# Banded attention feeding a gated feed-forward: product with v joined to a later pair's scores, ungated weight loads, a table of rank shifts

## The chip, the cores and the metric

One Trainium2 chip, one core of it. The metric is device time in microseconds (us) of one launch, the median of the runs shown. One further execution was taken by the profiler; all rows come from that one.

## What is computed

Attention over 4 batches, 8 heads, 768 positions and head size 64, with a band (128 positions back) and 4 sink positions, followed by a gated feed-forward on 3072 tokens:

```python
scores = scale * np.matmul(q, k.transpose(0, 1, 3, 2))
keep = is_sink | in_window          # pos < 4, or 0 <= row - col < 128
a = softmax(where(keep, scores, -1e9))
x = (a @ v)  as [3072, 512]         # 8 heads of 64 side by side
out = (sigmoid(x @ w_gate) * (x @ w_val)) @ w_out     # 512 -> 1536 -> 512
```

The feed-forward's operands are each cut into a rounded part and a rest, so that a product takes three matrix multiplies (high by high, high by rest, rest by high). The weights arrive as 64-bit floats and are decoded on the chip.

## The kernel before, in words

**Order of the work.** `Plan` (from line 270) is a list scheduler that runs when the kernel is built. Each `plan.op` gives a rank (`prio`, lower goes first), the engines that may run it with a cost in ns, and the tiles that it reads and writes. `Plan.run` (299) plays time forward: when an engine is free it takes the waiting operation of lowest rank whose inputs are there and whose tiles have a free buffer (412). What it writes out is a fixed order of instructions for each engine: PE (TensorE), V (VectorE), A (ScalarE), G (GpSimd) and Q (the SP queue, which issues the DMAs in that order). On the chip each engine keeps to this order, and an instruction whose input is late holds all behind it. When PE has nothing it puts in filler multiplies with the identity (`warm`).

**Attention** works on pairs of heads and blocks of two 128-row tiles: 4 batches, 3 blocks each, 4 pairs each, 48 pairs in all. `u` counts heads in this order and goes up by two for a pair, so u = 28 is the 29th head. `attend` (841) plans one pair with rank u: three loads (k, q, v, from buffers with three places each), the scores on PE (900), masks and row minimum on V, exponentials on A, normalization on G or V, four transposes on PE (985), a copy on A and two masking selects on G into `wt`, and the product with v on PE (`pv`, 1038), whose two halves are copied by A and added by V into `xr`. Scores and `pv` use the array as four 64x64 tiles (`parts=True`); all else on PE uses it whole. The planner charges 150 and 210 ns for changing between the two and, while it is in tiles, looks first for other such operations. Scores take two PSUM banks of the pool `a`, `pv` takes two, a transpose one; the pool has four (`B_a`, 73).

**After each block** `join` (1068) adds the sinks' part and either cuts the block's 256 tokens into `XH`, `XL` for the first form of the feed-forward (`feed`, blocks 0, 1, 2 and 4, ranks of 10000 and over on PE), or writes it to DRAM (the other eight blocks, `SPILL`). These eight are computed once attention is over, by a second form (`wino`) that needs the banks of pool `a`.

**Weights.** There are 12 slices f, each of three matrices (`weights`, 1223). A matrix is one load of 512 KB into one of four raw buffers (`wst` three, `wsx` one) and a chain over A, V and G (`decode`, 1161). The n-th matrix has rank DS + DR n, that is 6.0 + 0.3 n. `GATES` says at which head a slice may start to load: slice 0 after the normalizer (`guard`, 955) of u = 0, the other eleven after that of u = 6, by a dependence through the marker `OPEN`.

Of the kernel before, what the change touches and what calls it, by code (L numbers as in the profile page):

```python
# [40 lines left out]
SINKU = 2  # L41
# [4 lines left out]
DEEP = 3  # L46
SCALP = -0.5
SKSWAP = 0
GATES = ((2, 1), (8, 11))
MORE_W = 1  # L50
DS = 6.0
DR = 0.3
ALT = 1
SURE = 600.0
# [23 lines left out]
B_w = 2  # L78
B_m = 2
BUFS = {}  # L80

@with_exitstack
def general(ctx, tc, q, k, v, ident, nsk, win, wres, wol_d, out):
# [391 lines left out]
def kernel(  # L475
# [362 lines left out]
            lambda: vs()[2 * NR : 3 * NR], [raw], [vs],  # L838
        )

    def attend(u, b, h, t0, T, XS, PSK):

        prev = 1 if t0 else 0
        L = T + prev
        W = T * 128
        if u == SINKU if b == 0 else h == 0 and t0 == 0:
            sinks(b, u)
        at = (b * NT + t0) * H + h * T
        own = u < 2 * H and u // 2 % 2
# [50 lines left out]
        def scores():  # L900
# [10 lines left out]
                            skip_group_check=True, tile_position=(e * D, c * D),  # L911
                        )

        plan.op(
            u, [("PE", 10 + sum(1.67 * (KW + D if t0 + t else KW) for t in range(T)), scores)],
            [qkT, qr], sc + [P], soon=soon, parts=True,
        )
        for e in range(2):

            def pick(e=e):  # L920
                def tiles(at):
                    x = sc[e]()[:, at + SIDE * (T - n) : at + SIDE * (T - n) + 128]
                    return bass.AP(x.tensor, x.offset, (x.ap[0], (SIDE, n), (1, 128)))

                V.copy_predicated(
                    out=tiles(0), mask=tri.unsqueeze(1).to_broadcast([128, n, 128]), data=tiles(KW)
                )

            n = T if t0 else T - 1
            plan.op(u, [("V", 170.0 + 135.0 * n, pick)], [(MASKS, 3)], [sc[e]])  # L930
            for t in range(T):

                def top(e=e, t=t):
                    V.tensor_tensor_reduce(
                        out=Pv()[:, e, t], in0=sc[e]()[:, t * SIDE : t * SIDE + KW],
                        in1=am[min(t0 + t, 2)], op0=ALU.add, op1=ALU.min, scale=-SCALE,
                        scalar=3.0e38,
                        accum_out=negm_all[:, at + e * T + t : at + e * T + t + 1],
                    )

                def exp(e=e, t=t):
                    A.activation(
                        out=Pv()[:, e, t], in_=Pv()[:, e, t], func=AF.Exp,
                        bias=negm_all[:, at + e * T + t : at + e * T + t + 1], scale=-1.0,
                        accum_out=sums()[:, e * T + t, 0:1],
                    )

                plan.op(
                    u, [("V", 330, top)],
                    [sc[e]] + [(MASKS, x) for x in ((0,), (1, 4), (2, 4))[min(t0 + t, 2)]],  # L950
                    [(P, (e, t))],
                )
                plan.op(u, [("A", 495, exp)], [], [(P, (e, t)), (sums, (e, t))])
# [84 lines left out]
        def pv():  # L1038
            for i, (l, halves) in enumerate(blocks):
# [8 lines left out]
                            tile_position=(z * D, e * D),  # L1048
                        )

        plan.op(
            u, [("PE", 15 + sum(1.67 * max(x[2] for x in hs) for _, hs in blocks), pv)],
            [vt, wt], sides + [(xst, c)], parts=True,
        )
        plan.op(
            u, [("A", act(W, True), lambda: A.copy(out=xs()[:, c], in_=sides[0]()[:, 0:W]))],
            [sides[0]], [(xst, c)],
        )
        plan.op(
            u, [("V", vec(W), lambda: V.tensor_tensor(  # L1060
                out=xs()[:, c], in0=sides[1]()[:, 0:W], in1=xs()[:, c], op=ALU.add
            ))],
            [sides[1]], [(xst, c)],
        )
        if h == H - 2:
            join(u + 1, b, t0, T, XS, psk)

    def join(u, b, t0, T, XS, psk):

        W, vs = T * 128, VSP  # L1070
        spill, g = place[b, t0]
        first = u == H - 1
        bank = (
            lambda: Tile(OS, None, F32, "eO", len(OS)) if first
            else Tile(AS, None, F32, "a", len(AS))
        )
        u -= AHEAD if first else 0
        ts = bank()
        sk = tile([3 * NR, W], F32R, "sk", BUFS["sk"], pa)

        def turn():
            for t in range(T):
                PE.transpose(
                    out=ts()[0:NR, t * 128 : t * 128 + 128],
                    in_=psk()[:, t].rearrange("p h s -> p (h s)"), identity=ident,
                )

        n = turn_of.get("sk", 0)
        turn_of["sk"] = n + 1
        plan.op(u, [("PE", 20 + T * 100, turn)], [psk], [ts, sk]).turn = "sk", n  # L1090
        for i in (0, 2):
            plan.op(
                u, [("A", act(W, True), lambda i=i: A.copy(
                    out=sk()[i * NR : i * NR + NR], in_=ts()[0:NR, 0:W]
                ))],
                [ts], [(sk, i)],
            )
        rest(
            u, W, lambda: sk()[NR : 2 * NR], lambda: ts()[0:NR, 0:W], lambda: sk()[0:NR],
            [ts, (sk, 0)], [(sk, 1)], True,  # L1100
        )
        runs = [] if spill else [[0]]
        for t in range(1, 0 if spill else T):
            if chunk_of[g + t] == chunk_of[g + t - 1]:
                runs[-1].append(t)
            else:
                runs.append([t])
        for i, xst in enumerate(XS):
            xs = lambda xst=xst: xst().rearrange("p (c x) -> p c x", c=2)
            for cc in ((0,), (1,)) if T == 3 else ((0, 1),):  # L1110
                C = len(cc)
                sp = bank()
                spv = lambda sp=sp, C=C: sp()[:, 0 : C * W].rearrange("p (c x) -> p c x", c=C)

                def add(i=i, spv=spv, cc=cc):
                    for c in cc:
                        PE.matmul(
                            spv()[:, c - cc[0]], lhsT=vs()[:, 2 * i + c], rhs=sk(), start=True,
                            stop=True,
                        )  # L1120

                plan.op(u, [("PE", C * mac(W), add)], [vs, sk], [sp])
                mine = [(xst, c) for c in cc]
                cut = slice(cc[0], cc[-1] + 1)
                plan.op(
                    u, [("V", vec(C * W), lambda spv=spv, xs=xs, cut=cut: V.tensor_tensor(
                        out=xs()[:, cut], in0=spv(), in1=xs()[:, cut], op=ALU.add
                    ))],
                    [sp], mine,
                )  # L1130
                if spill:
                    dma(
                        u, 728.0, lambda n=g // 2, i=i, xst=xst: Q.dma_start(out=x_d[n, i], in_=xst()),
                        mine, [(XD, (g // 2, i))],
                    )
                for run in runs:
                    cols = slice(run[0] * 128, run[-1] * 128 + 128)
                    k = (g + run[0]) % RING * 128
                    ts_ = slice(k, k + len(run) * 128)
                    fs = slice(2 * i + cc[0], 2 * i + cc[-1] + 1)  # L1140
                    parts = [(2 * i + c, (g + t) % RING) for t in run for c in cc]
                    x = lambda cols=cols, xs=xs, cut=cut: xs()[:, cut, cols]
                    hi = lambda ts_=ts_, fs=fs: XH()[:, fs, ts_]
                    lo = lambda ts_=ts_, fs=fs: XL()[:, fs, ts_]
                    n = C * len(run) * 128
                    copy(u, n, hi, x, mine, [(XH, p) for p in parts], C == 1 and len(run) % 2)
                    rest(
                        u, n, lo, x, hi, mine + [(XH, p) for p in parts], [(XL, p) for p in parts]
                    )
# [595 lines left out]
                    weights(next(decoded), due)  # L1745

    opened(0)
    u = g = fed = ci = 0
    for b in range(B):
        t0 = 0  # L1750
        for T in AT[b]:
            XS, PSK = [], [None]
            for h in range(0, H, 2):
                attend(u, b, h, t0, T, XS, PSK)
                if u >= MIX0 and (u - MIX0) % MIXD == 0 and (u - MIX0) // MIXD < 2 * NP:
                    mixed(u + 0.5, (u - MIX0) // MIXD)
                for _ in range(2):
                    u += 1
                    opened(u)
            if not place[b, t0][0]:  # L1760
                g += T
            t0 += T
            while ci < len(MT) and fed + sum(MT[ci]) <= g:
                feed(ci, fed, MT[ci])
                fed += sum(MT[ci])
                ci += 1
    for i in range(WT):
        wino(ci + i, 4 * i)
    plan.run(WARM, 218.0, warm)
    wres = {f: [w() if i < 4 else w()[:, 0] for i, w in enumerate(ws)] for f, ws in wres.items()}  # L1770

# [79 lines left out]
```

## Time and profile before

| | us |
|---|---|
| median of 3 runs | 739.62 (739.58 to 740.27) |
| profiled execution | 739.36 |
| its span on the core | 737.6 |
| granted TensorE clock, mean | 1.0 of full speed |

The profiled execution's time exceeds the span by 1.8 us of launch and end. The page's rows give busy time by engine; a start-to-start distance between two PE rows says more about PE than its busy share, since matmuls overlap each other.

### The profile page before, as it was taken

The page shows a single profiled execution, that of the slowest core. Times are in us where ns is not written, and L with a number is a line of the kernel's source. Part 1 is how long each engine was busy: PE and PEld are TensorE (multiplying, and loading weights), DVE is VectorE, ACT ScalarE, POOL GpSimd, SP SyncE. Part 2 cuts the span into 40 slices and gives each one's busy share as a digit, 9 for nine tenths or more (in the row PEclk, how much of TensorE's full clock was granted, in tenths as well). Part 3 has the DMA queues.
Part 4 walks back from the last instruction along what each step waited for, and adds up shares of the span by engine and source line. Part 5 has one row for each costly group of instructions (what it writes and reads, how often), then busy time and mean ns, then how long its engine had stood idle before and what let it go on. Part 6 is the DMA issues. An engine that isn't in the chain of part 4 may idle for free.

```text
span 737.6 us, 16836 instructions
## 1 busy us (share of the span) xinstructions
PE 722.3 (98%) x6264; PEld 646.6 (88%) x6264; DVE 400.9 (54%) x1121; ACT 374.2 (51%) x1029; POOL 430.0 (58%) x433
## 2 busy tenths in 40 slices
PE   7999999999999999999999999999999999999997
PEld 6788787888888888899899999999999999999996
DVE  5999998787868766532242354424543334443231
ACT  6988886566656656522233344433444334343332
POOL 3879887999999646510154455644556445554331
PEclk9999999999999999999999999999999999999999
DMA  8768885666767754432245233453334432353312
GB/s 260 259 224 256 289 277 166 215 188 189 224 211 243 237 156 124 140 118 66 77 128 170 88 100 117 146 171 98 99 114 145 161 112 89 120 149 93 122 44 74
DMA packets 71769, 115.43 MB, mean 156 GB/s; under 512 B 7300, under 2 KB 31876, under 8 KB 71684
## 3 DMA queue, kind: packets, MB, share of 16 engines
q1 hardware_dynamic: 71680, 114.32, 49.5%
q8 instruction: 50, 0.82, 0.4%
q14 instruction: 35, 0.29, 0.2%
q10 hardware_dynamic: 4, 0.00, 0.0%
HBM read 94.37 MB, written 19.92 MB: 155 GB/s over the span
## 4 chain that ended last, share of the span: by engine, by line
PE 75%; POOL 10%; DVE 6%; ACT 6%; issue 3%; DVEq 0%; POOLq 0%; ACTq 0%
PE a L531 41%; PE m L531 19%; PE o L531 14%; POOL wst L531 5%; POOL wt L531 2%; DVE a L531 1%; POOL P L531 1%; ACT a L531 1%; ACT P L531 1%; DVE w L531 1%; DVE P L531 1%; DVE xr L531 1%; POOL graw L531 1%; ACT ep L531 0%; ACT wst L531 0%
## 5 line engine op out<-in xcount | busy, mean ns | idle before, releaser
L531 POOL TENSOR_TENSOR tt<-tf,tt 128x512 fp32r<-128x512 f32 x75 | 96.8, 1300 | 127.8 <-ACT tt L531 113.7
L531 DVE TENSOR_TENSOR a<-a,big 128x256 f32<-128x256 f32 x72 | 31.1, 432 | 143.8 <-PE a L531 143.7
L531 PE MATMUL a<-xa,tt 128*128 128x256 f32 x672 | 102.4, 281 | 0.0
L531 PEld LDWEIGHTS a<-xa,tt 128*128 128x128 f32 x672 | 91.7, 188 | 1.9
L531 ACT ACTIVATE P<-P,negm_all 128x132 f32<-128x132 f32 x176 | 69.8, 398 | 23.7 <-DVE negm_all L531 23.3
L531 PE MATMUL o<-woh,graw 128*128 128x512 f32 x192 | 74.9, 409 | 0.0
L531 ACT CAST tt<-tf 128x512 fp32r<-128x512 f32 x67 | 41.6, 621 | 55.4 <-PE a L531 38.9
L531 POOL TENSOR_SCALAR_AFFINE_SELECT wt<-wt 128x512 f32<-128x512 f32 (+1 forms) x88 | 57.0, 651 | 13.4 <-ACT wt L531 10.2
L531 PE MATMUL m<-XH,wvh 128*128 128x256 f32 x216 | 61.7, 296 | 0.0
L531 PE MATMUL m<-XL,wvh 128*128 128x256 f32 x216 | 58.5, 281 | 0.0
L531 PE MATMUL m<-XH,wgh 128*128 128x256 f32 x193 | 57.1, 296 | 1.0 <-DVE traw L531 1.0
L531 PE MATMUL m<-XH,wvl 128*128 128x256 f32 x204 | 57.5, 282 | 0.0
L531 PE MATMUL m<-XH,wgl 128*128 128x256 f32 x192 | 54.4, 283 | 1.2 <-POOL wgl L531 1.2
L531 ACT ACTIVATE tf<-a 128x512 f32<-128x512 f32 x36 | 21.5, 598 | 65.7 <-DVE a L531 56.0
L531 PE MATMUL m<-XL,wgh 128*128 128x256 f32 x192 | 54.0, 281 | 0.0
L531 POOL TENSOR_TENSOR XH<-tf,XH 128x512 fp32r<-128x512 f32 x16 | 20.8, 1298 | 42.8 <-ACT XH L531 31.0
L531 PEld LDWEIGHTS m<-XH,wvh 128*128 128x128 f32 x216 | 40.0, 189 | 5.6 <-issue 3.1
L531 PEld LDWEIGHTS o<-woh,graw 128*128 128x128 f32 x192 | 36.2, 188 | 7.8 <-issue 1.7
L531 POOL TENSOR_TENSOR XL<-tf,XL 128x512 fp32r<-128x512 f32 x12 | 16.9, 1405 | 44.6 <-ACT XL L531 44.6
L531 DVE SCALAR_TENSOR_TENSOR traw<-traw,m 128x256 f32<-128x256 f32 x48 | 20.0, 416 | 40.2 <-PE m L531 36.4
L531 PEld LDWEIGHTS m<-XH,wgh 128*128 128x128 f32 x193 | 36.5, 189 | 5.4 <-issue 1.7
L531 DVE TENSOR_TENSOR xr<-a,xr 128x256 f32<-128x256 f32 (+1 forms) x70 | 34.4, 499 | 11.2 <-ACT xr L531 9.8
(239 smaller groups left out, 2163.2 us busy)
## 6 DMA issues: line engine op xcount, KB each, us to landing
tf<-tw_d SPq DMA_DIRECT2D x96, 256.0 KB, 2.7
wol<-wol_d SPq DMA_DIRECT2D x84, 256.0 KB, 3.0
tw_d<-wst SPq DMA_DIRECT2D x24, 256.0 KB, 2.6
qkT<-in_k_dram SPq DMA_DIRECT2D x30, 198.0 KB, 3.2
v<-in_v_dram SPq DMA_DIRECT2D x30, 192.0 KB, 2.9
qr<-in_q_dram SPq DMA_DIRECT2D x44, 128.0 KB, 3.5
out_dram<-w SPq DMA_DIRECT2D x20, 256.0 KB, 2.8
wst<-in_moe_w_gate_dram SPq DMA_DIRECT2D x9, 512.0 KB, 5.4
```

Source lines behind the costliest of these rows:

```text
L531: return lambda *a, **kw: tc.keep_in_program_order(op(*a, **kw))
```

## The change

- `GATES` becomes ((0, 12),): all twelve slices are planned ahead of the first head, and no load of theirs waits on `OPEN`.
- From u = 28 on (`MERGE0`) `attend` returns a function `rear` that plans the product with v and what follows. It is kept in a list, and from u = 36 on (`MERGE0 + 2 * LAG`) the oldest one is taken out and plans one PE operation: the product with v of pair u - 8, then the scores of pair u. The last four rears come alone. The sinks' load of a later batch and the end of a block (`join`, `feed`) move into `rear`.
- In `join` the PE add of the sinks' part waits, for u over 28, for the block's `xr` as well.
- `DS` goes from 6.0 to 6.05; `TOP` gives a name to a cost that stays 330.
- A table `RANKS` of some 900 numbers is added to the ranks just before `Plan.run`: by engine (P, V, A, G, Q: first engine that may run it) and hundredths of rank for attention and weights, by twelfths of a slice for the feed-forward (mA, mG, mV, mQ, and M for its PE operations).

```diff
-GATES = ((2, 1), (8, 11))
+GATES = ((0, 12),)
 MORE_W = 1
-DS = 6.0
+MERGE0 = 28
+LAG = 4
+TOP = 330
+DS = 6.05
...
+RANKS = dict(
...
+    P={0: -2.135, 200: -0.861, 400: 2.898, 600: 0.927, 800: -5.684, 1000: 0.074, 1200: -0.858,
...
+    Q={0: -0.919, 100: 0.506, 200: -1.221, 300: -0.967, 400: -3.99, 450: -0.028, 500: 1.859,
+        600: -0.224, 605: 0.16, 635: 1.129, 665: -0.149, 695: -0.176, 700: -0.135, 725: 0.615,
+        755: 0.479, 785: -1.178, 800: 0.344, 815: -0.347, 845: -0.291, 905: 0.423, 935: -1.647,
...
+        1325: 0.174, 1355: 0.229, 1385: 0.921, 1400: -0.092, 1415: -1.048, 1445: 0.061, 1475:
+        3.156, 1505: 0.019, 1535: -1.497, 1565: 19.572, 1595: -0.513, 1600: -0.028, 1625: 0.608,
...
-    def attend(u, b, h, t0, T, XS, PSK):
+    def attend(u, b, h, t0, T, XS, PSK, back=None):
...
-        if u == SINKU if b == 0 else h == 0 and t0 == 0:
+        if b == 0 and u == SINKU:
...
+        cost = 10 + sum(1.67 * (KW + D if t0 + t else KW) for t in range(T))
+        if back is None:
+            plan.op(u, [("PE", cost, scores)], [qkT, qr], sc + [P], soon=soon, parts=True)
+        else:
+            back(scores, cost, [qkT, qr], sc + [P])
...
+        def rear(more=None, cost=0.0, r=(), w=()):
+
+            if b and h == 0 and t0 == 0:
+                sinks(b, u)
+
+            def both_kinds():
+                pv()
+                if more:
+                    more()
+
+            plan.op(
+                u, [(
+                    "PE", 15 + sum(1.67 * max(x[2] for x in hs) for _, hs in blocks) + cost,
+                    both_kinds,
+                )],
+                [vt, wt] + list(r), sides + [(xst, c)] + list(w), parts=True,
+            )
...
+            if h == H - 2:
+                join(u + 1, b, t0, T, XS, psk)
+                joined(b, t0, T)
+
+        return rear
...
+                plan.op(
+                    u, [("PE", C * mac(W), add)], [vs, sk] + (mine if u > MERGE0 else []), [sp]
+                )
...
+                back = rears.pop(0) if u >= MERGE0 + 2 * LAG else None
+                rear = attend(u, b, h, t0, T, XS, PSK, back)
+                if u >= MERGE0:
+                    rears.append(rear)
+                else:
+                    rear()
...
+    for o in plan.ops:
+        e, pr = o.ways[0][0][0], o.prio
+        if 0 <= pr < 100:
+            o.prio += RANKS.get(e, {}).get(round(pr * 100), 0.0)
+        elif -1000.5 < pr < -900:
+            o.prio += RANKS.get("m" + e, {}).get(round((pr + 1000) * 12), 0.0)
+        elif 10000 <= pr < 11000:
+            o.prio += RANKS.get("M", {}).get(round((pr - 10000) * 24), 0.0)
     plan.run(WARM, 218.0, warm)
```

## Rows read from the trace of the kernel before

**Rows 1.** The page, part 1: busy us (share of the span) and instructions.

```profile
PE 722.3 (98%) x6264; PEld 646.6 (88%) x6264; DVE 400.9 (54%) x1121; ACT 374.2 (51%) x1029; POOL 430.0 (58%) x433
```

**Rows 2.** Stretches: busy of PE, PEld, DVE, ACT, POOL; clock; DMA share, GB/s.

```profile
0.00:20.00 20.00, 15.99 (x172) 13.17 (x176) 11.65 (x72) 13.07 (x44) 5.91 (x21) 1.00 0.84 263
20.00:120.00 100.00, 94.01 (x930) 79.95 (x920) 96.50 (x255) 85.01 (x227) 84.01 (x89) 1.00 0.79 252
120.00:310.00 190.00, 189.67 (x2235) 161.66 (x2234) 133.33 (x541) 118.88 (x446) 156.60 (x187) 1.00 0.63 191
310.00:366.00 56.00, 55.55 (x392) 50.94 (x391) 15.05 (x31) 13.16 (x32) 4.99 (x4) 1.00 0.31 94
```

**Rows 3.** Groups of PE instructions, 0 to 120 us: busy us, mean ns, idle before.

```profile
L531 PE MATMUL m<-ident 128*128 128x128 f32 x170 | 25.6, 297 | 3.0 <-POOL ident masks.py:199 1.8 <-DVE traw L531 1.1
```

**Rows 4.** Timeline of PE: start, length; scores alone, product with v alone.

```profile
293.21 0.89 PE L531 MATMUL a<-qkT,qr 64*64 64x196 f32 x16
294.04 0.38 PE L531 MATMUL m<-XH,wvh 128*128 128x256 f32 x1
...
295.64 0.89 PE L531 MATMUL a<-wt,v 64*64 64x192 f32 x24
296.46 0.50 PE L531 MATMUL o<-woh,graw 128*128 128x512 f32 x1
```

**Rows 5.** Timeline of PE: product with v and scores next to each other.

```profile
231.08 0.28 PE L531 MATMUL m<-XL,wgh 128*128 128x256 f32 x1
231.20 0.28 PE L531 MATMUL m<-XH,wgl 128*128 128x256 f32 x1
231.41 0.89 PE L531 MATMUL a<-wt,v 64*64 64x192 f32 x24
232.12 0.84 PE L531 MATMUL a<-qkT,qr 64*64 64x196 f32 x16
232.89 0.39 PE L531 MATMUL m<-XH,wvh 128*128 128x256 f32 x1
233.11 0.28 PE L531 MATMUL m<-XL,wvh 128*128 128x256 f32 x1
```

**Rows 6.** Timeline of PE: first and last of 50 runs in tiles from u = 28 on.

```profile
116.39 0.79 PE L531 MATMUL a<-qkT,qr 64*64 64x132 f32 x16
...
304.26 0.89 PE L531 MATMUL a<-wt,v 64*64 64x192 f32 x24
```

**Rows 7.** Timeline of DVE behind rows 5: it empties the four banks.

```profile
233.09 0.41 DVE L531 TENSOR_TENSOR xr<-a,xr 128x256 f32<-128x256 f32 x1
233.42 0.74 DVE L531 COPY_PREDICATED a<-tri,a 128x256 f32<-128x256 int32 x2
...
234.94 0.08 DVE L531 DVE_READ_ACCUMULATOR2_ANT negm_all<- 128x1 f32 x1
```

**Rows 8.** Stretch 120 to 310 us, scores alone (tile qkT): PE, PEld; clock, DMA.

```profile
120.00:310.00 190.00, 26.89 (x528) 17.65 (x528) 1.00 0.63 191
```

**Rows 9.** Timeline of the SP queue: start and length of DMA issues.

```profile
6.69 0.47 SPq L531 DMA_DIRECT2D qkT<-in_k_dram  x1
...
11.09 0.42 SPq L531 DMA_DIRECT2D wst<-in_moe_w_gate_dram  x1
...
17.23 0.38 SPq L531 DMA_DIRECT2D v<-in_v_dram  x1
20.99 0.38 SPq L531 DMA_DIRECT2D ev<-in_v_dram  x1
21.42 0.46 SPq L531 DMA_DIRECT2D wsx<-in_moe_w_gate_dram  x1
```

**Rows 10.** DMA issues by line: size, median us from issue to landing.

```profile
wst<-in_moe_w_gate_dram SPq DMA_DIRECT2D x9, 512.0 KB, 5.4
```

**Rows 11.** Timeline of DVE: idle time before the instruction in brackets.

```profile
13.59 0.16 DVE L531 TENSOR_REDUCE rs<-sums 128x4 f32<-128x8 f32 x1 [1.14 <-ACT ep L531]
16.65 0.49 DVE L531 COPY_PREDICATED o<-tri,o 128x128 f32<-128x128 int32 x2 [1.39 <-PE o L531]
```

**Rows 12.** Timeline of PE: the first matmul of the feed-forward.

```profile
40.27 0.36 PE L531 MATMUL m<-XH,wgh 128*128 128x256 f32 x1
```

More of the change, by code (lines that the diff above doesn't have):

```diff
@@ L80 @@
 BUFS = {}
+RANKS = dict(
+    A={0: -0.207, 10: 0.182, 200: -4.396, 400: -4.3, 600: -1.602, 605: -0.418, 635: -0.259, 665:
[13 rows of a table added]
+    G={0: -0.764, 200: 2.58, 400: 2.405, 450: -5.588, 600: -0.234, 605: -0.587, 635: 0.011, 665:
[13 rows of a table added]
+    M={0: 0.072, 1: 0.19, 2: 0.178, 3: 0.051, 4: 0.616, 5: -0.224, 7: -0.008, 8: 0.241, 9:
[11 rows of a table added]
+    P={0: -2.135, 200: -0.861, 400: 2.898, 600: 0.927, 800: -5.684, 1000: 0.074, 1200: -0.858,
[8 rows of a table added]
+    Q={0: -0.919, 100: 0.506, 200: -1.221, 300: -0.967, 400: -3.99, 450: -0.028, 500: 1.859,
[15 rows of a table added]
+    V={0: -0.013, 10: 4.252, 200: 1.54, 400: -0.691, 600: 1.199, 605: 2.306, 635: -3.73, 665:
[13 rows of a table added]
+    mA={0: 0.152, 1: 0.046, 2: 1.287, 4: -0.006, 5: -0.108, 6: 0.078, 7: -0.437, 8: 0.083, 9:
[10 rows of a table added]
+    mG={0: -0.228, 2: 0.043, 3: -0.415, 4: -0.334, 5: 0.021, 6: -0.331, 8: -0.011, 9: -0.209,
[9 rows of a table added]
+    mQ={12: -0.021, 13: -0.322, 14: 0.013, 15: 0.493, 16: 1.273, 17: -0.161, 18: -0.089, 19:
[9 rows of a table added]
+    mV={0: -0.092, 1: 0.126, 2: 1.484, 3: 0.058, 4: -0.418, 5: 0.114, 6: 0.011, 7: -0.098, 8:
[8 rows of a table added]
+)
 @with_exitstack
@@ L912, in scores @@
                         )
[L914 to L917, printed above, removed]
+        cost = 10 + sum(1.67 * (KW + D if t0 + t else KW) for t in range(T))
[3 more added lines that the diff above has]
+            back(scores, cost, [qkT, qr], sc + [P])
         for e in range(2):
@@ L948, in attend @@
                 plan.op(
-                    u, [("V", 330, top)],
+                    u, [("V", TOP, top)],
                     [sc[e]] + [(MASKS, x) for x in ((0,), (1, 4), (2, 4))[min(t0 + t, 2)]],
@@ L1049, in pv @@
                         )
[L1051 to L1066, printed above, removed]
+        def rear(more=None, cost=0.0, r=(), w=()):
[13 more added lines that the diff above has]
+            plan.op(
+                u, [("A", act(W, True), lambda: A.copy(out=xs()[:, c], in_=sides[0]()[:, 0:W]))],
+                [sides[0]], [(xst, c)],
+            )
+            plan.op(
+                u, [("V", vec(W), lambda: V.tensor_tensor(
+                    out=xs()[:, c], in0=sides[1]()[:, 0:W], in1=xs()[:, c], op=ALU.add
+                ))],
+                [sides[1]], [(xst, c)],
+            )
+            if h == H - 2:
+                join(u + 1, b, t0, T, XS, psk)
+                joined(b, t0, T)
+        return rear
     def join(u, b, t0, T, XS, psk):
@@ L1120, in add @@
                         )
-                plan.op(u, [("PE", C * mac(W), add)], [vs, sk], [sp])
                 mine = [(xst, c) for c in cc]
+                plan.op(
+                    u, [("PE", C * mac(W), add)], [vs, sk] + (mine if u > MERGE0 else []), [sp]
+                )
                 cut = slice(cc[0], cc[-1] + 1)
@@ L1747, with joined, feeds @@
     opened(0)
-    u = g = fed = ci = 0
+    state = dict(g=0, fed=0, ci=0)
+    ended = []
+    def joined(b, t0, T):
+        ended.append((b, t0, T))
+    def feeds():
+        if not ended:
+            return
+        b, t0, T = ended.pop()
+        if not place[b, t0][0]:
+            state["g"] += T
+        while state["ci"] < len(MT) and state["fed"] + sum(MT[state["ci"]]) <= state["g"]:
+            feed(state["ci"], state["fed"], MT[state["ci"]])
+            state["fed"] += sum(MT[state["ci"]])
+            state["ci"] += 1
+    u, rears = 0, []
     for b in range(B):
@@ L1753 @@
             for h in range(0, H, 2):
-                attend(u, b, h, t0, T, XS, PSK)
+                back = rears.pop(0) if u >= MERGE0 + 2 * LAG else None
[4 more added lines that the diff above has]
+                    rear()
                 if u >= MIX0 and (u - MIX0) % MIXD == 0 and (u - MIX0) // MIXD < 2 * NP:
@@ L1759 @@
                     opened(u)
-            if not place[b, t0][0]:
-                g += T
+                feeds()
             t0 += T
[L1763 to L1766, printed above, removed]
+    for rear in rears:
+        rear()
+        feeds()
+    ci = state["ci"]
     for i in range(WT):
         wino(ci + i, 4 * i)
+    for o in plan.ops:
[6 more added lines that the diff above has]
+            o.prio += RANKS.get("M", {}).get(round((pr - 10000) * 24), 0.0)
     plan.run(WARM, 218.0, warm)
```

105 rows, old and new, of tables (A, G, M, P) are left out of this document.

## The prediction

> **What bounds the kernel now.** I read the page first: PE is busy for 98% of the span [rows 1], so the span is PE's work plus what PE loses, and the change removes no matmul but fillers. Then the stretches by stage [rows 2] show where PE loses anything. From 310 us on it is dense and nothing of the change lies there but shifted ranks. From 120 to 310 us PE is also full (189.67 of 190), while DVE has 133, ACT 119 and POOL 157 of 190: PE bounds, and a gain there is shorter PE time alone. Before 120 us it is otherwise: DVE is busy 96.50 of 100 us between 20 and 120, ACT and POOL 85 and 84, and PE's 94 is partly fillers: 170 of them, 25.6 us, all before 120 us [rows 3]. There attention and the weights' decoding bound, on DVE first, and PE waits for decoded slices; whatever lets the decoding end earlier moves all of PE's later work forward. The granted clock is full in every stretch.
>
> **Part 1, product with v and scores in one operation.** Instructions stay the same, their neighbours change. Scores alone hold PE for 294.04 - 293.21 = 0.83 us to the next whole-array matmul, the product with v alone for 0.82 [rows 4]. Next to each other both take 232.89 - 231.41 = 1.48 [rows 5], so a shared run saves 0.17. A run also costs on its way in and out: a whole-array matmul follows another after 0.12, the first tiled one comes 0.21 behind its forerunner, and the second whole one after the run 0.22 behind the first [rows 5], together 0.19 more. A run saved is worth 0.17 + 0.19 = 0.36 us.
>
> How many are saved? From u = 28 on there are 34 score operations and 35 products with v (one left from u = 26), and they stand in 50 runs [rows 6]: the planner joins 19 of the 69 already. Afterwards there are 1 + 4 + 30 + 4 = 39 operations, the four first scores, 30 joint ones and four last products included. Two joint ones can't easily stand next to each other, since each takes all four banks of pool a. So 11 runs go: 11 x 0.36 = 4.0 us. Ends: 13 runs if the first scores pair up, 4.7; and nothing if the joint operation comes late where the two parts would have come at leisure. I take 4.0, since PE is the bound in that stretch and each saved run shortens it directly.
>
> What the joint operation waits for: product u - 8 now waits until the scores of u may go (k, q, a place in P, four banks). In the trace it runs about that late anyway: the last of 34 products starts at 304.26, and a pair passes every (304.3 - 116.4) / 34 = 5.5 us [rows 6]; 528 score matmuls, 16 to an operation, make 33 operations in 190 us [rows 8]. Behind it on PE stand feed-forward products, ordered in only when the planner thinks that the joint one is ready. Its followers (ACT's copy, DVE's add, the block's join, SP's spill writes, and the load of v into the freed place) move along with it; the new wait in `join` holds one PE add until the block's xr is done. Their cover is the stretch from 310 to 366 us, where DVE has 15 and POOL 5 of 56 [rows 2] and PE still has feed-forward to do: attention may end up to that much later at no cost. So nothing is charged. Without that cover each us of delay would cost one.
>
> Emptying the four banks takes DVE from 233.09 to 235.02, 1.9 us, of a pair's 5.5 [rows 6, 7], so I charge no wait for it. The Trainium skill, "TensorEngine Tiling (Array Packing)", section Performance Considerations, warns that tiling makes TensorE faster but not the emptying of PSUM, which may become the bottleneck. By that rule the joint operation would wait for its banks, part 1 would give nothing, and the sum would be 4.0 us worse; by the row it doesn't bind. No run here shows a joint operation that needs all four at once.
>
> **Part 2, loads that wait for no unit.** The first weight load is issued at 11.09, behind loads of six pairs [rows 9]. With ranks 6.05, 6.35, 6.65, 6.95 (shifted by the table to between 6.2 and 7.5) the first four come behind four pairs' loads only, where u = 8 (8.3) and u = 10 stand now: at about 6.7, so 4.4 us earlier, and the fourth no longer waits until 21.42 behind v loads whose buffers are full. Moved past them are six loads of u = 8 and 10. A weight load lands after 5.4 us [rows 10], at about 12.1 instead of 16.5. DVE is idle for 1.14 us before 13.59 and 1.39 before 16.65 [rows 11]; decoding can fill these 2.5 us. Since DVE is full from then on, and the first feed-forward matmul comes only at 40.27 [rows 12], what is done in these gaps comes off the decode-bound stretch: 2.5 us. Ends: 4.4 (the whole head start) and 0 (xr of block 0, not weights, sets the 40.27); a loss only if the six loads moved back come too late, 1 us by the same rows. I take 2.5, the gaps that the rows show.
>
> **Part 3, the table, and DS.** No row shows what 900 shifted ranks do. What order alone can win is bounded by idle time: between 20 and 120 us DVE has 3.5, ACT 15, POOL 16 us idle [rows 2], 34.5 together, a third of it 11.5 if work were shared out perfectly over three engines. What it can lose: a queue that stops behind a full buffer, as SP does from 17.23 to 20.99 [rows 9], 3.8 us. One visible entry shows the risk: rank 15.65, a weight load of slice 10, is sent back by 19.6. I take a gain of 3.5, DVE's own idle time, being the nearest to the bound engine. The gate's write by `guard` was a dependence without an instruction: zero. The sinks' load in `rear` is planned later but keeps its rank; it is needed at the block's join only: zero. `TOP` changes nothing.
>
> **Sum.** 739.36 - 4.0 - 2.5 - 3.5 = 729.4 for the profiled execution; the median of the runs stands 0.26 above that execution, so 729.6 us.
>
> **Rivals.** *A, most of it was there already.* Product and scores are already neighbours in 19 cases, the planner and not the chip may like the new order, and only the early loads pay: 739.6 - 2.5 = 737.1. For it: PE has no visible gaps from 120 us on; against it: 0.36 per run is plain in the rows. *B, the table orders queues wrongly for the chip.* Engines keep the planned order, so a load planned for a place that comes free late holds the decode loads behind it for 3.8 us [rows 9]. One such hold in the DVE-bound stretch, with parts 2 and 3 lost to it and part 1 kept, gives 739.6 - 4.0 + 3.8 = 739.4; two give 743.2. *C, slower: the four banks set the pace.* If a pair's cycle grows past 5.5 + 56 / 30 = 7.4 us, attention ends behind the feed-forward that covers it, and the second form, which needs these banks, starts late. At 8.0 us a pair that is 30 x 0.6 = 18 us more: 739.6 - 6.0 + 18 = 751.6. Against it: all of DVE's work of a pair, 133.33 / 34 = 3.9 us [rows 2], and the joint run's 1.5 make 5.4, well below 7.4. The rule of the Trainium skill named above, from "TensorEngine Tiling (Array Packing)", Performance Considerations, speaks for this rival; the rows so far speak against it.
>
> **How the numbers follow.** Forecast 0.68 (its own range 722 to 736), A 0.14, B 0.10 (of which 0.06 at one hold, 0.04 at two), C 0.08. A difference under 0.2%, 1.5 us, can't be told from none here. Forecast and A are faster: 0.82. One hold is no change: 0.06. Two holds and C are slower: 0.12. The range goes from 721 (the further ends of parts 2 and 3 in part) to 740, with A and one hold in it, and leaves out C, two holds and the far end of the table's gain.
>
> **What would show it.** Part 1: some 39 runs in tiles from u = 28 on, and joint runs of about 1.5 us; attention ending between 290 and 330 us with PE full to the end. Part 2: the first weight load near 6.7 us, the fourth right behind it, and the first feed-forward matmul some 2 to 3 us before 40.27. Part 3: fewer than 25.6 us of fillers, and PE waits that don't grow. It is wrong if fillers or PE waits appear between 120 and 366 us (C), if SP stands for several us ahead of weight loads between 20 and 120 (B), or if the time falls by much more than 10 us, which would mean that order alone shortened the DVE-bound stretch by more than DVE's own gaps.

## The result and the profile after

The changed kernel takes 732.53 us (median of 4 runs, 730.98 to 732.76) against 739.94 for the kernel before (739.58 to 740.63): 0.9894 of the time, 95% interval 0.9877 to 0.9911, or 7.4 us less. Forecast were 729.6 us, 721 to 740. Run again in a later set of runs (e12, below) it took 730.56. Its profiled execution took 732.44 us, its span is 730.6.

The page, part 1, of the changed kernel: busy time, share and instructions of each engine.

```profile
PE 714.6 (98%) x6234; PEld 641.9 (88%) x6234; DVE 404.2 (55%) x1125; ACT 370.9 (51%) x1024; POOL 433.2 (59%) x434
```

PE has 30 instructions fewer than in [rows 1], and the fillers are 30 fewer than in [rows 3], so nothing else went and no record is missing:

```profile
L655 PE MATMUL m<-ident 128*128 128x128 f32 x140 | 22.3, 304 | 2.0 <-POOL ident masks.py:199 1.8 <-ACT traw L655 0.2
```

The stretches of [rows 2], changed kernel (busy of PE, PEld, DVE, ACT, POOL; granted clock; DMA share, GB/s):

```profile
0.00:20.00 20.00, 16.52 (x173) 13.83 (x174) 13.16 (x75) 15.00 (x49) 9.59 (x26) 1.00 0.86 275
20.00:120.00 100.00, 92.74 (x948) 77.50 (x947) 93.49 (x270) 84.34 (x233) 85.36 (x93) 0.98 0.79 252
120.00:310.00 190.00, 189.20 (x2084) 163.94 (x2083) 133.66 (x498) 106.77 (x399) 135.48 (x158) 1.00 0.60 186
310.00:366.00 56.00, 56.00 (x544) 52.09 (x543) 27.60 (x72) 24.94 (x72) 22.23 (x23) 1.00 0.44 130
```

Three things stand out. PE is still full from 120 us on, so the joint operation cost next to no waits. Attention's work on DVE, ACT and POOL has moved into the stretch from 310 to 366 us, and PE stays full there too. And the mean clock between 20 and 120 us is 0.98, where [rows 2] have 1.00.

The timeline of PE, a joint operation of the changed kernel (start, length), to be held against [rows 5]:

```profile
231.32 0.28 PE L655 MATMUL m<-XH,wvl 128*128 128x256 f32 x1
231.53 0.89 PE L655 MATMUL a<-wt,v 64*64 64x192 f32 x24
232.24 0.84 PE L655 MATMUL a<-qkT,qr 64*64 64x196 f32 x16
233.01 0.39 PE L655 MATMUL m<-XH,wgh 128*128 128x256 f32 x1
233.24 0.28 PE L655 MATMUL m<-XL,wgh 128*128 128x256 f32 x1
```

It takes 233.01 - 231.53 = 1.48 us, its way in 0.21 and its way out 0.23, to a hundredth what the chance neighbours of before took. The first and the last of 38 runs in tiles from u = 28 on, changed kernel (50 before, [rows 6]):

```profile
101.13 0.79 PE L655 MATMUL a<-qkT,qr 64*64 64x132 f32 x16
...
333.61 1.55 PE L655 MATMUL a<-wt,v 64*64 64x192 f32 x48
```

The last run holds two last products (x48), and attention ends 29 us later than before. The timeline of the SP queue and of PE's first feed-forward matmul, changed kernel, for [rows 9, 12]:

```profile
7.16 0.47 SPq L655 DMA_DIRECT2D wst<-in_moe_w_gate_dram  x1
...
8.65 0.63 SPq L655 DMA_DIRECT2D wsx<-in_moe_w_gate_dram  x1
9.32 1.32 SPq L655 DMA_DIRECT2D qkT<-in_k_dram  x1
...
35.11 0.36 PE L655 MATMUL m<-XH,wgh 128*128 128x256 f32 x1
```

The first weight load goes 3.9 us earlier, the fourth right behind it, and the first feed-forward matmul comes 5.2 us earlier than in [rows 12].

**A ledger for all kernels.** Where the time went can be read off PE alone, since PE is full from 125 us on. Three sums per profiled execution, each over all PE rows of its timeline:

- *Work done by 125 us*: every matmul that has started by then, fillers left out, at its start-to-start price in the kernel before after 125 us (128x256: 0.120 us, 128x512: 0.2345, 128x128: 0.10, a 64x64 one 0.033; the few other shapes likewise). A us more done is a us less to do.
- *Runs in tiles after 125 us*, at the 0.36 us that the prediction gave to one.
- *The last matmul's start*, which the first two should move.

The PE row of the stretch from 0 to 125 us (PE busy, instructions; clock; DMA share, GB/s), one kernel to a fence; before, then changed:

```profile
0.00:125.00 125.00, 114.93 (x1149) 1.00 0.78 249
```

```profile
0.00:125.00 125.00, 114.19 (x1159) 0.99 0.78 249
```

Less fillers these are 979 and 1019 matmuls. The runs of the next section are named here by their labels; all differences are to before.

| kernel | matmuls by 125 us, no fillers | work done, us | runs after 125 us | both, us | last matmul, us |
|---|---|---|---|---|---|
| before | 979 | 76.4 | 48 | | 733.09 |
| after | 1019 | +1.2 | -16 | -7.0 | -7.1 |
| e12, the same again | 1035 | +3.0 | -16 | -8.8 | -8.9 |
| e1 joint operation alone | 979 | 0 | -13 | -4.7 | -5.4 |
| e9 thirteen joint operations | 979 | 0 | -5 | -1.8 | -2.5 |
| e10 products held for three pairs | 979 | 0 | -13 | -4.7 | -4.0 |
| e2 early loads alone | 947 | -2.4 | +2 | +3.2 | +2.4 |
| e8 the same, behind six pair loads | 999 | +1.0 | +2 | -0.3 | -1.3 |
| e4 both, without the table | 957 | -1.2 | -13 | -3.4 | -5.3 |
| e11 as e4, loads as e8 | 998 | +0.9 | -13 | -5.6 | -5.6 |
| e3 loads and table, no joint operation | 1028 | +2.2 | +1 | -1.8 | -2.6 |
| e6 table's attention half | 1028 | +2.3 | -15 | -7.7 | -9.0 |
| e7 table's feed-forward half | 958 | -1.1 | -12 | -3.2 | -3.5 |
| e5 the changed kernel and five fillers | 1036 | +3.1 | -16 | -8.9 | -9.1 |

The two sums give the last matmul of both profiles of the changed kernel to 0.1 us, and that of the others to within 1.9 us, 0.8 us off on average. They leave out single stops of PE (below), and that a step's price varies. The 0.1 us is luck in part: behind 125 us the changed kernel loses about 1.0 us in two stops and before loses as much in two others, so what the sums leave out cancels. A run that starts before 125 us instead of after it counts as gone, though the kernel still has it. Nor is the last matmul the end: from there the spans have 4.6 us left, but 5.6, 6.0 and 5.8 in e1, e4 and e6. The row of e2 holds 1.2 us that belong to its one execution (below). The profiled executions come from several chips, on which before's median ranged from 739.94 to 740.47, so the verdicts below rest on the timed medians, and the ledger tells why.

### The profile page after: what moved, and what is told of

Same layout as the page of the kernel before. It is cut to its first block, busy times and chain, and to the rows that moved or that the text cites. A ratio compares the mean times of both kernels' runs of the same rounds, so it can differ in the third digit from the quotient of the medians.

```text
span 730.6 us, 16741 instructions
## 1 busy us (share of the span) xinstructions
PE 714.6 (98%) x6234; PEld 641.9 (88%) x6234; DVE 404.2 (55%) x1125; ACT 370.9 (51%) x1024; POOL 433.2 (59%) x434
## 4 chain that ended last, share of the span: by engine, by line
PE 83%; DVE 7%; ACT 3%; POOL 2%; issue 2%; DMA 2%; SPq 1%; DVEq 0%; POOLq 0%; ACTq 0%
PE a L655 44%; PE m L655 22%; PE o L655 17%; DVE a L655 2%; DVE w L655 2%; DMA wsx<-in_moe_w_gate_dram 1%; SPq L655 1%; ACT P L655 1%; ACT a L655 1%; DVE wst L655 1%; DMA qr<-in_q_dram 1%; DVE wol L655 0%; POOL P L655 0%; DVE traw L655 0%; POOL wst L655 0%
## 5 line engine op out<-in xcount | busy, mean ns | idle before, releaser
L655 POOL TENSOR_TENSOR tt<-tf,tt 128x512 fp32r<-128x512 f32 x79 | 105.1, 1336 | 89.7 <-ACT tt L655 74.7
L655 PE MATMUL a<-xa,tt 128*128 128x256 f32 x600 | 91.3, 281 | 0.0
L655 PEld LDWEIGHTS a<-xa,tt 128*128 128x128 f32 x600 | 82.2, 189 | 2.0
L655 POOL TENSOR_SCALAR_AFFINE_SELECT wt<-wt 128x512 f32<-128x512 f32 (+1 forms) x88 | 60.6, 690 | 22.7 <-ACT wt L655 19.4
L655 ACT CAST tt<-tf 128x512 fp32r<-128x512 f32 x72 | 44.6, 620 | 53.8 <-PE a L655 28.0
L655 POOL TENSOR_TENSOR XH<-tf,XH 128x512 fp32r<-128x512 f32 x19 | 25.4, 1337 | 38.6 <-ACT XH L655 30.6
L655 DVE COPY_PREDICATED a<-tri,a 128x256 f32<-128x256 int32 (+1 forms) x86 | 29.8, 385 | 27.1 <-PE a L655 26.9
L655 PEld LDWEIGHTS m<-XL,wvh 128*128 128x128 f32 x216 | 40.4, 191 | 0.5
L655 PEld LDWEIGHTS a<-wt,v 64*64 64x64 f32 x944 | 30.8, 133 | 11.1 <-POOL wt L655 3.0
L655 DVE CUSTOM_DVE_ANT_0 P<-a,am 128x132 f32<-128x132 f32 x164 | 40.3, 288 | 0.1
```

What stands on the lines that cost most here:

```text
L655: return lambda *a, **kw: tc.keep_in_program_order(op(*a, **kw))
```

## The experiments

Every kernel here computes the whole reference. Medians and ratios are against the kernel before, run in between on the same chip.

| run | us | before | ratio (95%) | difference |
|---|---|---|---|---|
| e1 | 734.98 | 740.47 | 0.9924 (0.9910 to 0.9938) | -5.5 |
| e2 | 740.62 | 740.47 | 1.0000 (0.9991 to 1.0009) | +0.2 |
| e3 | 737.59 | 740.47 | 0.9965 (0.9950 to 0.9979) | -2.9 |
| e4 | 735.80 | 740.47 | 0.9935 (0.9921 to 0.9949) | -4.7 |
| e5 | 731.19 | 740.18 | 0.9880 (0.9865 to 0.9896) | -9.0 |
| e6 | 731.69 | 740.18 | 0.9885 (0.9869 to 0.9900) | -8.5 |
| e7 | 736.29 | 740.18 | 0.9951 (0.9938 to 0.9965) | -3.9 |
| e8 | 739.16 | 740.18 | 0.9983 (0.9974 to 0.9991) | -1.0 |
| e9 | 737.24 | 740.41 | 0.9958 (0.9944 to 0.9971) | -3.2 |
| e10 | 736.04 | 740.41 | 0.9937 (0.9924 to 0.9950) | -4.4 |
| e11 | 733.54 | 740.41 | 0.9903 (0.9890 to 0.9916) | -6.9 |
| e12 | 730.56 | 740.41 | 0.9872 (0.9857 to 0.9886) | -9.9 |

### The parts one by one: e1, e2, e3, e4

e1, the joint operation alone (edit against the changed kernel):

```diff
-GATES = ((0, 12),)
+GATES = ((2, 1), (8, 11))
-DS = 6.05
+DS = 6.0
-RANKS = dict(
...
+RANKS = {}
```

> The joint operation alone, without the ungated loads and without the table. Theory of the prediction: 11 runs in tiles fewer from u = 28 on at 0.36 us, so 4.0 us less than before, about 735.9 us, with 39 such runs and the first feed-forward matmul still near 40.3 us. Rival (the table does all, the planner had joined them already): within 1 us of before, 739 to 741 us. Rival (banks set the pace): slower than before.

Measured -5.5 us. Up to 125 us the kernel does what before did, to the matmul; all of the gain is behind that. 13 runs went, not 11: two of the first four scores and two of the last four products stand together as well (the last run of e1 is an x48 as in the changed kernel). Over all PE rows from 125 us on, the tiled matmuls and the steps into and out of them take 61.41 us start to start in before and 54.65 in e1, while 13 more whole-array steps at 0.143 come in: 61.41 - 54.65 - 1.86 = 4.9, or 0.38 us for a run. Rival A, by which the planner had most of it already, falls.

e2, the early loads alone:

```diff
-MERGE0 = 28
+MERGE0 = 1000
-RANKS = dict(
...
+RANKS = {}
```

> The ungated loads and DS 6.05 alone. Theory of the prediction: 2.5 us less than before, about 737.4 us, first weight load near 6.7 us and the first feed-forward matmul 2 to 3 us before 40.3. Rival (xr of the first block, not the weights, sets the first feed-forward matmul; loads gain nothing): within 1 us of before.

Measured nothing (0.9991 to 1.0009), though the loads went at 7.17 and the first feed-forward matmul came at 35.88 instead of 40.27. The stretch row shows that the work done falls behind, 32 matmuls fewer at 125 us even with fillers (168) left out:

```profile
0.00:125.00 125.00, 114.64 (x1115) 1.00 0.77 246
```

Part of that belongs to this one execution, which took 741.79 us, the slowest of e2's eleven and 1.2 above their median. PE stayed longer at half pace in it. The fillers ahead of the scores of u = 2, timeline of PE, before, then e2:

```profile
1.76 3.78 PE L531 MATMUL m<-ident 128*128 128x128 f32 x16 [1.76 <-POOL ident masks.py:199]
7.29 2.27 PE L531 MATMUL m<-ident 128*128 128x128 f32 x18
```

```profile
7.29 4.03 PE L535 MATMUL m<-ident 128*128 128x128 f32 x18
```

Before's fillers take half the time from 7.3 us on, those of e2 only from 11 us on. (The clock column gives 1.00 for these first microseconds in both, which the fillers contradict.) e4, below, does the same work as e2 on every engine, in the same order, up to 134 us, and its 18 filler rows there take the usual 2.27 us. It runs 1.0 us ahead of e2 from 16 us on and 1.2 at 125 us, and lacks 22 matmuls there instead of 32. So what the early loads do is read from e4.

The scores of the next two pairs come late. The timeline of PE, before, then e4 (the tile ek is u = 10's, the second row's qkT is u = 8's):

```profile
16.96 0.85 PE L531 MATMUL a<-ek,eq 64*64 64x196 f32 x16
19.46 0.89 PE L531 MATMUL o<-qkT,qr 64*64 64x196 f32 x16
```

```profile
21.32 0.89 PE L535 MATMUL o<-qkT,qr 64*64 64x196 f32 x16
23.45 0.89 PE L535 MATMUL a<-ek,eq 64*64 64x196 f32 x16
```

Those of u = 8 come 1.9 us later and those of u = 10 6.5, because their k and q now follow 2 MB of weights. The stretches from 10 to 20 us and from 0 to 40, before, then e4 (columns as in the stretches above):

```profile
10.00:20.00 10.00, 7.75 (x118) 5.91 (x114) 6.52 (x41) 7.37 (x32) 4.65 (x8) 1.00 0.97 324
0.00:40.00 40.00, 34.73 (x393) 28.75 (x394) 31.42 (x132) 31.90 (x100) 23.54 (x41) 1.00 0.82 263
```

```profile
10.00:20.00 10.00, 8.16 (x111) 6.24 (x104) 7.24 (x41) 8.76 (x36) 7.67 (x11) 1.00 0.94 324
0.00:40.00 40.00, 35.32 (x365) 29.28 (x366) 29.70 (x129) 31.22 (x99) 22.77 (x40) 1.00 0.79 255
```

The DMA engines were busy to 0.97 already, and they move the same 324 GB/s in either kernel: an early weight load displaces another transfer. DVE, whose gaps were to be filled, is busy for 7.24 us instead of 6.52: of the two gaps in [rows 11] one shrinks, from 1.39 to 0.34 us,

```profile
16.78 0.49 DVE L535 COPY_PREDICATED o<-tri,o 128x128 f32<-128x128 int32 x2 [0.34 <-PE o L535]
```

and the other is still there with 1.25. Behind 20 us DVE loses more than that: by 40 us it has been busy for 29.70 us instead of 31.42. That the late scores are what leaves it idle is not shown. In the changed kernel, whose loads stand as early, the same scores start later still, at 20.52 and 25.24, and under the table DVE has been busy for 31.28 us by 40 us.

e3 (loads and table, no joint operation) and e4 (joint operation and loads, no table):

```diff
-MERGE0 = 28
+MERGE0 = 1000
```

> The changed kernel without the joint operation: loads and table stay. If the parts add up as predicted it loses the joint operation's 4.0 us: about 736.5 us. Rival (the table was fitted to the joint order and harms without it): at or above before, 740 us or more. Rival (the table does all): within 1 us of the changed kernel, 732 to 733.5.

```diff
-RANKS = dict(
...
+RANKS = {}
```

> The changed kernel with an empty table: joint operation and ungated loads stay. Theory of the prediction: loses the table's 3.5 us, about 736 us. Rival (the table does all): 739 to 741. Rival (the table costs time on the chip, by the loads held back or the clock that fell to 0.66 from 55 to 60 us): below the changed kernel, 731 us or less.

e3 gains 2.9 us, so against e2 the table is worth 3.0 without a joint operation. e4 gains 4.7, 0.8 less than e1: added to the joint operation the early loads do harm, which is the work missing at 125 us (957 matmuls against 979). The three parts thus give -5.5, +0.8 and the rest, -2.7, to make -7.4.

### Which part of the table: e6, e7

```diff
+    for key in ("M", "mA", "mG", "mQ", "mV"):
+        RANKS[key] = {}
     for o in plan.ops:
```

> The changed kernel with only the half of the table that shifts attention and weights (A, G, P, Q, V). Theory (order before 120 us is where the table pays, for weights, attention and DVE's gaps): nearly all of its 3 us stay, 732 to 733.5 us. Rival (the shifts inside the feed-forward pay): about 735.5 us, as without the table.

```diff
+    for key in "AGPQV":
+        RANKS[key] = {}
     for o in plan.ops:
```

> The changed kernel with only the half of the table that shifts the feed-forward (M, mA, mG, mQ, mV). Theory (the table pays by attention and weights): within 1 us of the kernel without a table, 735 to 736.5 us. Rival: about 732.5 us.

With the ranks of attention and weights alone (e6) the time is 731.69, no slower than the whole table's 732.53; with those of the feed-forward alone (e7) it is 736.29, no better than without a table. The gain is in the first half, and the ledger says how: e6 has 70 matmuls more done by 125 us than e7, 3.5 us of work, and 3 runs fewer after 125 us. The fillers show it too, 140 against 168.

### The order of the loads: e8, e11

e8 is e2 with the weight loads behind k, q and v of u = 8 and 10; e11 is e4 with the same edit:

```diff
-        n = next(staged) % (3 + MORE_W)
+        k = next(staged)
+        n = k % (3 + MORE_W)
+        load = max(prio, 10.05 + 0.01 * k)
...
-        plan.op(prio, [("Q", 460, lambda: Q.dma_start(out=words(), in_=src))], [OPEN, DECODED], [st], dma=1456.0)
+        plan.op(load, [("Q", 460, lambda: Q.dma_start(out=words(), in_=src))], [OPEN, DECODED], [st], dma=1456.0)
```

> Ungated loads alone, as in the second experiment, but no weight load is ranked ahead of the k, q and v loads of u = 8 and 10. Theory (the head start of the weights gained nothing because it held back these six loads, and scores of u = 8 came 5 us late): scores of u = 8 start near 17 us again and the time is 1 to 2.5 us below before, 738 to 739.5. Rival (what decodes earlier only moves work, DVE is as full as before up to the end of decoding): within 1 us of before.

> Joint operation and ungated loads without the table, and the weight loads ranked behind the k, q and v loads of u = 8 and 10. Theory (parts add up): 5.5 us of the joint operation and 1 us of the loads, about 733.7 us, 2 us below the kernel with no table. Rival (the loads' order decides nothing once products are joined): about 735.8 us as there.

The timeline of PE, e8:

```profile
16.84 0.85 PE L535 MATMUL a<-ek,eq 64*64 64x196 f32 x16
19.29 0.89 PE L535 MATMUL o<-qkT,qr 64*64 64x196 f32 x16
...
32.88 0.36 PE L535 MATMUL m<-XH,wgh 128*128 128x256 f32 x1
```

The scores stand where they stood in before (the expectation of e8 gave u = 8 the place near 17, which is u = 10's), the weight loads still go a little earlier than in before (10.16 against 11.09) and all four in a row, and the first feed-forward matmul comes at 32.88, earlier than in e2. The stretch row:

```profile
0.00:125.00 125.00, 113.04 (x1163) 1.00 0.78 251
```

With 164 fillers left out that is 999 matmuls, 52 more than e2; and e11 has 998, 41 more than e4, so most of this is not that execution's own. e8 gains 1.0 us where e2 gained none, and e11 gains 6.9 where e4 gained 4.7, so the order of six small loads against four large ones is worth 1 to 2 us, and the missing gate at most 1.4 (e11 against e1). So the order of the loads is the cause: put back the k and q, and the work is back. The same edit under the table was not tried.

### The size of the joint part: e9, e10

Both are e1 with one number changed: joint operations in the last 13 pairs only, and products held back for three pairs instead of four.

```diff
-MERGE0 = 28
+MERGE0 = 62
```

> The joint operation alone as in the first experiment, but from u = 62 on: 13 joint operations instead of 30. Theory (a fixed price for each run in tiles that goes, some 13 runs and 4.6 us for 30 joint ones, the rest of the 5.5 us from the passage to the second form): 13/30 of the runs go, 5 or 6, and the time is about 2 to 3 us below before, 737.5 to 738.5. Rival (the gain comes from attention ending later, at 341 instead of 305 us, and is there as soon as some products are joined): 735 to 736.

```diff
-LAG = 4
+LAG = 3
```

> The joint operation alone, but the product with v of u - 6 stands with the scores of u. Theory (its inputs are ready only about four pairs after its own scores, so scores now wait for them; attention slows down but stays covered by the feed-forward up to 366 us): attention ends later than with a lag of four, and the time is that of the first experiment within 1.5 us, 734.5 to 736.5. Rival (a pair's cycle passes 7.4 us and the cover is gone): PE waits or fillers after 120 us and more than 738 us.

e9 loses 5 runs and gains 3.2 us (2.1 to 4.1), more than the 1.8 of its runs; e10 loses 13 like e1 and gains 4.4. What differs is where PE stops, above all in its passage into the second form. The timelines of PE, before, then e1, then e9, then e10 (idle time ahead of the row in brackets; no row of the changed kernel or of e9 has one at the passage):

```profile
363.67 0.98 PE L531 MATMUL a<-XH,tt 128*128 128x256 f32 x6 [0.45 <-ACT m L531]
372.69 0.51 PE L531 MATMUL a<-xa,wvh 128*128 128x256 f32 x2 [0.17 <-DVE tf L531]
```

```profile
213.30 0.47 PE L535 MATMUL a<-sk,vsp 96*128 96x256 f32 x2 [0.69 <-DVE xr L535]
...
351.95 0.38 PE L535 MATMUL m<-XH,wvh 128*128 128x256 f32 x1 [0.21 <-ACT traw L535]
```

```profile
210.36 0.89 PE L535 MATMUL a<-wt,v 64*64 64x192 f32 x24 [0.60 <-POOL wt L535]
```

```profile
351.01 0.38 PE L535 MATMUL m<-XH,wvh 128*128 128x256 f32 x1 [0.24 <-ACT traw L535]
...
358.94 0.75 PE L535 MATMUL a<-XL,tt 128*128 128x256 f32 x4 [0.86 <-POOL tt L535]
```

Before stops twice, both times at the passage: its matmul ahead of 363.67 starts at 362.84, 0.83 earlier where 0.12 is usual, so 0.71 is lost, and 0.34 at the second stop. e9 loses none of this 1.05 but stops for 0.60 elsewhere, so 1.8 + 1.05 - 0.6 = 2.3 are found of the 2.5 us by which its last matmul comes earlier; the rest of the timed 3.2 us is not. In e1 the stops give nothing on balance: less is lost at the passage, and 0.69 us at 213.30, where the add of the sinks' part waits for DVE's `xr`, as the new wait in `join` asks. e10 waits at the passage for POOL, since its attention ends later still (last product at 346.65 against 340.43 in e1), when the second form wants its inputs, which leaves 4.0 of the 4.7 us of its runs.

### The clock: e5, e12

In the changed kernel's profile PE's clock falls once (last section). e5 puts five fillers, ten rows of the trace, into the second of the two stops ahead of it; e12 is the changed kernel once more.

```diff
-                plan.op(
+                o = plan.op(
                     u, [("PE", C * mac(W), add)], [vs, sk] + (mine if u > MERGE0 else []), [sp]
                 )
+                o.fills = 5 if u == 15 and i == 0 else 0
...
         for o, e, fn in order:
+            for _ in range(getattr(o, "fills", 0)):
+                fill()
             fn()
```

> The changed kernel with five filler multiplies put in front of the PE add that stood idle for 1.26 us until 55.32 us; nothing else moves. Theory (the clock at half from 56.3 to 59.8 us costs what the one run at a mean clock of 0.999 was faster, 1.6 us): the clock stays full and the time is about 731 us where the changed kernel takes 732.5. Rival (PE waits there for DVE anyway, the clock costs nothing): 732 to 733 with a full clock. If the clock falls in spite of the fillers, nothing is told.

> The changed kernel itself once more, beside before on the same chip, to set the fillers and the halves of the table against. 732 to 733 us with the clock at half for some 3.5 us near 57 us, or about 731 where the clock stays full.

e5 kept the clock and took 731.19. But e12, without them, took 730.56 and kept it too in its profile, so the fillers are not shown to have done it. No version was found that is surely faster than the changed kernel: e5 and e6 lie between its own two medians (730.56 and 732.53).

## Why the prediction was right

The median and the signs were right, and two of the three terms; the sum hides one term that was wrong.

**Part 1, 4.0 forecast, 5.5 measured: right, and under-sized.** The price of a run held (0.36; 0.38 in e1), as did the joint run's 1.48 us. The count failed: "11 runs go" was 13 in e1, the end of the range that the prediction named for the case that first scores pair up, and 12 in the changed kernel (50 to 38); 13 x 0.36 = 4.7. The two stops at the passage stood in no row that the prediction read. The new wait in `join`, which it put at nothing, cost e1 0.69 us, so the 0.8 us between 4.7 and 5.5 are not found in stops and stay open. Nothing was charged for the later end of attention, on the cover from 310 to 366 us. That held: attention ended at 334 us, past the 290 to 330 that the prediction named as a sign, and PE stayed full. Rival C falls by the same rows: a pair's cycle did grow, from 5.5 to some 6.5 us (30 joint operations from 132.05 to 319.82 us), but stayed under the 7.4 from which it decides. e10 shows the edge of this cover: where attention ended near 347 us, PE waited at the passage.

The Trainium skill, "TensorEngine Tiling (Array Packing)", section PSUM Bottleneck, spoke for rival C: tiles make TensorE faster and not the copying out of PSUM, which may then bound. No run here bears it out: from 125 us on the changed kernel's PE waits twice, for 0.30 and 0.35 us, and neither wait is a joint operation's. The timeline of PE, changed kernel:

```profile
129.55 0.50 PE L655 MATMUL a<-sk,vsp 96*128 96x256 f32 x2 [0.30 <-DVE sk L655]
...
184.56 0.39 PE L655 MATMUL m<-XH,wgh 128*128 128x256 f32 x1 [0.35 <-DVE traw L655]
```

**Part 2, 2.5 forecast, nothing measured: wrong.** The step that failed is "decoding can fill these 2.5 us" of DVE's gaps. The loads went early (7.16, forecast 6.7) and the feed-forward began 5 us early, more than the 2 to 3 forecast. But DVE filled only 0.7 us of its gaps by 20 us, and by 40 us it had done 1.7 us less work than before (e4). The loss by "the six loads moved back", which the prediction put at 1 us at most, took the whole gain, and 0.8 us more beside the joint operation: on a DMA that was full already, scores of two pairs came 1.9 and 6.5 us late, and with the loads put back the work was back (e8, e11). The row that would have told is the DMA share of 0.97 between 10 and 20 us, printed by the same view that gave [rows 2], only in a finer stretch. A head start of one engine's first instruction is no gain by itself when the same transfers feed the work it is meant to overlap.

**Part 3, 3.5 forecast, 2.7 to 5.2 measured: right in size, by a bound.** Against e4, each by its difference to before on its own chip, the table gives 7.4 - 4.7 = 2.7, and 9.9 - 4.7 = 5.2 where the clock stayed full; 3.0 without the joint operation. As forecast, it shows in fillers (22.3 us against 25.6) and brings decoding and attention forward before 125 us: work done goes from -1.2 in e4 to +1.2, and to +3.0 with the full clock. The 16 runs against 13 in the ledger are no further saving: from u = 28 on the changed kernel has 38 runs and e1 37, but six of these against two start before 125 us. The 3.5 was an estimate from idle time, no mechanism; which entries of the table matter was found only as far as its half. Rival B, an SP queue that the table stops for several us, was not seen; what it described, loads in the wrong order, happened in part 2. One sign of part 3 missed: PE's idle time before 125 us did not stay but grew, from 10.1 to 10.8 us. And one reading was wrong, though no term hangs on it: the clock was not full in every stretch, for before's fillers run at half pace up to 7.3 us (e2).

**The sum.** Forecast 4.0 + 2.5 + 3.5 = 10.0. Measured 5.5 - 0.8 + 2.7 = 7.4 at first, and 9.9 in e12, for which the ledger finds 16 x 0.36 = 5.8 in runs and 3.0 in work done by 125 us. The nearness of 729.6 to 730.56 is two errors that offset, part 2 against parts 1 and 3.

## What to carry to other kernels

Where one engine is full, price a change by that engine's rows alone: steps between array forms times their start-to-start cost, plus the work that it has done when the full stretch begins; here two sums found the last matmul of the thirteen other profiles to 0.7 us on average, single stops left out. Before moving a large load ahead of small ones, look at the DMA share of the very stretch that it moves into: near 1.00, it takes their place rather than a gap. A longer chain off the bounding engine is free while the cover behind it lasts, and the passage to the next stage is where to look for its end.

## What was not expected: the clock at half speed for 3 us

In the changed kernel's profile PE stops twice near 54 us, by its rows until ACT has written sk, a tile of the sinks' part, and then until DVE has written w, a step of the weights' decoding. The timeline of PE, changed kernel (idle time in brackets):

```profile
53.43 0.63 PE L655 MATMUL a<-ident,P 128*128 128x128 f32 x4 [0.66 <-ACT sk L655]
55.32 0.84 PE L655 MATMUL a<-sk,vsp 96*128 96x256 f32 x4 [1.26 <-DVE w L655]
57.12 1.59 PE L655 MATMUL a<-qkT,qr 64*64 64x196 f32 x16
```

Two stretches of it, the one of the stops and the one behind (columns as above, the clock behind POOL's busy time):

```profile
52.50:55.50 3.00, 1.08 (x17) 0.73 (x10) 2.94 (x4) 2.86 (x8) 1.50 (x2) 1.00 0.81 277
56.50:59.50 3.00, 3.00 (x24) 2.06 (x23) 2.58 (x7) 2.35 (x5) 2.93 (x4) 0.50 0.62 191
```

Behind the stops the granted clock is 0.50 of full speed, that is 1.2 GHz, and a group of 16 score matmuls takes 1.59 us. The same stretches of e12, the same kernel in a later set of runs, and its PE rows:

```profile
52.50:55.50 3.00, 1.17 (x26) 0.82 (x18) 2.90 (x5) 2.86 (x8) 1.76 (x2) 1.00 0.79 284
56.50:59.50 3.00, 3.00 (x35) 2.57 (x34) 3.00 (x9) 2.07 (x4) 2.93 (x4) 1.00 0.79 221
```

```profile
53.70 0.63 PE L655 MATMUL a<-ident,P 128*128 128x128 f32 x4 [0.66 <-ACT sk L655]
55.59 0.85 PE L655 MATMUL a<-sk,vsp 96*128 96x256 f32 x4 [1.26 <-DVE w L655]
57.03 0.90 PE L655 MATMUL a<-qkT,qr 64*64 64x196 f32 x16
```

The stops are equal to a hundredth, 0.66 and 1.26 us, and the clock stays at 1.00, 2.4 GHz. The price is 732.44 - 730.61 = 1.8 us between the two profiled executions, and the ledger's work done by 125 us differs by the same 1.8. As e12 stands 0.27 us behind at both stops, the lower clock took some 2.1 us. Single runs of either set went the other way: 730.98 at a mean clock of 0.999 among three near 732.6 at 0.996, and 732.16 among three near 730.5. The Trainium skill, "TensorE: Matmul & The Clock Gate", section What's actually happening, says that the clock is halved according to how busy the engine has been; the changed kernel's rows agree with that, and e12's show that equal stops need not bring it about. What decides between the two was not settled: e5's fillers shortened the second stop, and the clock stayed full as it did in e12 without them.
